# Second MLP of a fused attention and two-MLP kernel: stores moved to GpSimd's queue, weight requests reordered, lower halves of split operands made later

## The chip, the cores and the metric
The kernel runs on one core of a Trainium2 chip. The metric is the device time of one execution in microseconds (us), median of several runs. TensorE (PE; its weight loads are PEld), VectorE (DVE), ScalarE (ACT) and GpSimd (POOL) each work through a queue of their own in order. SyncE (SP) computes nothing: its queue holds requests for transfers (DMA). A request that waits for a semaphore holds back all requests behind it on its queue. The transfers themselves run on the core's 16 DMA engines.

## The reference, cut to what matters
```
x  = attention(q, k, v)            # 4 x 576 tokens = 2304, 512 wide
h1 = x @ w1_in                     # first MLP, d_ff 2048
y  = (h1 - tanh(h1)) @ w1_out
h2 = y @ w2_in                     # second MLP: this is where the change is
g  = h2 * tanh(softplus(h2))       # Mish
out = g @ w2_out
```
All is float32. The kernel reaches float32 precision on TensorE by splitting each operand into an upper half (what is left after rounding to a shorter format) and a lower half (the difference), and by three products: upper x upper, upper x lower, lower x upper. The upper half comes from ScalarE (a copy, or Mish itself, written in the short format), the lower half from a subtract on DVE.

## The kernel before, in words
The second MLP uses Strassen-like 2x2 block products. The 2304 tokens are four blocks u = 0 to 3: 768 tokens, then three times 512. The 2048 hidden columns are eight slices j = 0 to 7. A group k = 8u + j handles one slice for one block; there are 32, one after the other. A group has seven products with W2in's block j (`product`, line 1052; six matmuls each, in the order 2, 0, 1, 4, 3, 5, 6 from block 1 on), each followed by some of the second-layer units of the group before (`o2_units`: 12 of three matmuls in block 0, seven of six matmuls after it, named 11, 22, S1, S3, 12, S2, S4). `UNITS` (line 1298) says how many units follow which product. Behind each product stand the steps of `combine` (line 1110): ScalarE or DVE take the product from one of two PSUM banks (products 2, 4, 6 in one; 0, 1, 3, 5 and unit S4 in the other), add, apply Mish, and split the result into halves (`mish`, `halved`).

While block 0 runs (groups 0 to 7), the weights are prepared beside it by `w2_cycles` (line 165). Raw float64 rows are loaded (`load_raw`), joined to float32, summed and split. The products' operands W2in go to DRAM by `keep` (line 241, 1.8 MB in two stores a slice, tensor w2s), the sums for W2out by `t_lo` (line 223, four stores of 256 KB a slice, tensor w2t). From block 1 on each group loads W2in's block for the next group (`w2c_load`, line 332, two loads of 1024 and 768 KB, tile P) and W2out's sums for its own slice (`t_load`, line 342, four loads of 256 KB, tile w). P has buffers for two groups.

The outputs of a block of tokens leave at its end: block 0 by `o_evict` (line 1177, six stores), the others by `out_sums` (line 1213: adds on DVE, four stores). All these requests are on SP's queue, in the order in which the code stands. The operands of the next block are made by `y_prep` (line 960) in steps spread over some groups.

The whole second MLP stands in a stretch whose order is exactly the order of the code (line 1328). `group` (line 1301) emits a product, its units, then asks `bg2` (line 1511) for what runs beside it, and then `parts` takes turns between `combine` and these, from yield to yield; a yield is thus a place where another stream's instruction may come between. `bg2` gets the place p of the product in its group, 0 to 6. These lines set the places of the loads:
```
if u and p == 0:
    t_load(j)
if k + 1 >= NJ and k + 1 < NU * NJ and p == 1:
    w2c_load((k + 1) % NJ)
```

Of the kernel before, what the change touches and what calls it, by code (L numbers as in the profile page):

```python
# [15 lines left out]
ACTF = mybir.ActivationFunctionType  # L16
# [13 lines left out]
def kernel(  # L30
# [134 lines left out]
    def w2_cycles():  # L165
# [57 lines left out]
        def t_lo(j, i):  # L223
            if 0 <= j < NJ and (j, i) in ts_todo:
                ts_todo.remove((j, i))
                t, h = ts[j][i], TW[0][:, i, :]
                V.tensor_tensor(out=t.bitcast(F32R), in0=t, in1=h, op=ALU.subtract)
                for x, src in ((0, h), (1, t)):
                    nc.sync.dma_start(out=w2t[j][:, 2 * i:2 * i + 2, x, :], in_=src.rearrange("p (n c) -> p n c", n=2))

        def hi(W, i, src):
            A.activation(out=W[:, i:i + src.shape[1], 0, :], in_=src, func=ACTF.Copy)
# [8 lines left out]
        def keep(j):  # L241
            for q in range(2):
                n = 4 - q
                nc.sync.dma_start(out=w2s[j][q][:, 0:n, :], in_=f32(W2c[j][q][:, 0:n].rearrange("p n t c -> p n (t c)")))

        fetch("a", 0)
        fetch("b", 0)
# [712 lines left out]
    def y_prep(u):  # L960
        C = C3 if u else C2

        def load(kh, th):
            t = (p2["yl"].tile([128, 2, C2], F32, tag="yl", name="yl")[:, :, 0:C] if u and th else raw_f32()[
                :, 0:2 * C].rearrange("p (a n) -> p a n", a=2))
            n0 = 0
            while n0 < C:
                i, o = divmod(token0(u) + th * C + n0, HS)
                n = min(C - n0, HS - o)
                nc.sync.dma_start(out=t[:, :, n0:n0 + n], in_=ys[i][:, 2 * kh:2 * kh + 2, o:o + n])  # L970
                n0 += n
            return t

        def sub(o, x, y, op=ALU.subtract):
            V.tensor_tensor(out=o, in0=x, in1=y, op=op)  # L975

        def tile(p):
            if p < 6:
                if u == 0:
                    t = p2["yk"].tile([128, 2, 2, C2], F32R, tag="yk", name="yk")  # L980
                    Y[u, p] = [t[:, 0], t[:, 1]]
                elif u == 1:
                    t = p2["yk"].tile([128, 3, 2, C3], F32R, tag="yk", name="yk")
                    Y[u, p] = [t[:, 0], t[:, 1]]
                    free.append(t[:, 2])
                else:
                    if p == 2:
                        for n in ORDER[1][:-1]:
                            free.extend(Y[u - 1, n])
                    Y[u, p] = [free.pop(0) for _ in range(2)]  # L990
            elif u:
                if not Y6:
                    Y6.append(AT_p.tile([128, 2, 2, C3], F32R, tag="AT", name="AT"))
                    OUT.append(AT_p.tile([128, 2, 2 * C3], F32, tag="AT", name="AT"))
                Y[u, p] = [Y6[0][:, 0], Y6[0][:, 1]]
            else:
                Y[u, p] = [AT_p.tile([128, 2, C2], F32R, tag="AT", name="AT") for a in range(2)]

        def halves(p, t):
            if (u, p) not in Y:  # L1000
                tile(p)
            y = Y[u, p]
            for a in range(2):
                A.activation(out=y[a][:, 0, :], in_=t[:, a], func=ACTF.Copy)
                yield 0
                sub(y[a][:, 1, :], t[:, a], f32(y[a][:, 0, :]))

        a21, a22 = load(0, 1), load(1, 1)
        s1, s2 = [p2["yf"].tile([128, 2, C2], F32, tag="yf", name="yf")[:, :, 0:C] for _ in range(2)]
        yield 1  # L1010
        if u == 0:
            a11, a12 = load(0, 0), load(1, 0)
            for p in range(6):
                tile(p)
        sub(s1, a21, a22, ALU.add)
        yield 1
        if u:
            a11, a12 = load(0, 0), load(1, 0)
            yield 1
            sub(s2, s1, a11)  # L1020
            yield 1
            sub(a21, a11, a21)
            yield 1
            order = ((0, a11), (2, a12))[::1 if u == 1 else -1] + ((1, s2), (4, s1), (3, a21), (5, a22), (6, s2))
        else:
            yield from halves(5, a22)
            yield 1
            sub(a21, a11, a21)
            yield 0
            sub(s2, s1, a11)  # L1030
            yield 1
            order = ((3, a21), (0, a11), (1, s2), (2, a12), (4, s1), (6, s2))
        for p, t in order:
            yield from halves(p, t)
            if p == (1 if u else 2):
                sub(s2, a12, s2)
            yield 1


    ORDER = ((0, 2, 1, 4, 3, 5, 6), (2, 0, 1, 4, 3, 5, 6))  # L1040
    evict, YK, free = [], [], []
    Y6, OUT, TW, HB, Q, XG, late_sums, late_acc = [], [], [], [], {}, [], [], []

    def bank_of(k, p):
# [42 lines left out]
    def mish(k, n, src=None):  # L1087
        x = xs[k, n]
        h = x if src is None else src
        gg = operand(k, n)  # L1090
        A.activation(out=gg[:, 0, :], in_=h, func=ACTF.Mish)  # L1091
        A.activation(out=x, in_=h, func=ACTF.Mish)  # L1092
        yield 0
        V.tensor_tensor(out=gg[:, 1, :], in0=x, in1=f32(gg[:, 0, :]), op=ALU.subtract)  # L1094
        yield 0

    def halved(k, n, x):
        gg = operand(k, n)
        split(x, gg[:, 0, :], gg[:, 1, :], V)
        return 0  # L1100

    def sums_12(k):
# [7 lines left out]
    def combine(k, p):  # L1110
        t = bank_of(k, p)

        def add(o, x, y):
            V.tensor_tensor(out=o, in0=x, in1=y, op=ALU.add)  # L1114

        def keep(n):
            A.activation(out=x_of(k, n), in_=t, func=ACTF.Copy)  # L1117

        if p == 0:
            keep("11")  # L1120
        if p == (0 if k >= NJ else 2):
            add(xs[k, "11"], xs[k, "11"], bank_of(k, 2))
            yield from mish(k, "11")
        elif p == 1:
            keep("12")
            while late_sums:
                yield from late_sums.pop()
        elif p == 3:
            keep("22")
            add(xs[k, "22"], xs[k, "22"], bank_of(k, 4))  # L1130
            yield from mish(k, "22")
        elif p == 5:
            if k < NJ:
                x_of(k, "21")
                yield from mish(k, "21", t)
            else:
                y = x_of(k, "21")
                A.activation(out=y, in_=t, func=ACTF.Mish)
        elif p == 6:
            add(xs[k, "12"], xs[k, "12"], t)  # L1140
            while late_acc:
                late_acc.pop()()
            if k >= NJ:
                y = xs[k, "21"]
                add(xs[k, "22"], y, xs[k, "22"])
                yield from mish(k, "12")
                yield halved(k, "S1", xs[k, "22"])
                V.tensor_tensor(out=y, in0=xs[k, "11"], in1=y, op=ALU.subtract)  # L1148
                yield halved(k, "S3", y)
                late_sums.append(sums_12(k))  # L1150
            else:
                yield from mish(k, "12")
        yield 1

    def o2_units(k):
# [21 lines left out]
    def o_evict(u, tt):  # L1177
        o = p2["st"].tile([128, 512], F32, tag="y", name="y") if tt not in (5, 0) else OUT[0][:, tt // 5]
        if tt in (4, 1):
            V.tensor_copy(out=o, in_=ops[u, tt])  # L1180
        else:
            A.activation(out=o, in_=ops[u, tt], func=ACTF.Copy)
        nc.sync.dma_start(out=out[tt * 128:tt * 128 + 128, :], in_=o)

# [26 lines left out]
    def out_sums(u, n, j):  # L1213
# [4 lines left out]

        def store(o, th, ch):
            r0 = token0(u) + 2 * 128 * th  # L1220
            nc.sync.dma_start(out=out[r0:r0 + 256, C3 * ch:C3 * ch + C3].rearrange("(t p) c -> p t c", p=128),
                              in_=o.rearrange("p (t c) -> p t c", t=2))

        def staged(x, m):
# [100 lines left out]
    def pipeline(bg, bg2):  # L1325
        for s in range(0, SWITCH, 2):
            pair(s, bg)
        with tc.manual_schedule():
# [12 lines left out]
            for k in range(NU * NJ):  # L1341
                group(k, bg2)
            parts(late_sums)
            for _ in o2_units(NU * NJ - 1):
                pass
            late_acc.pop()()
# [55 lines left out]
    if True:  # L1402
# [109 lines left out]
        def bg2(k, p):  # L1512
            u, j = divmod(k, NJ)
            mix = []
            if u == 0:
                mix.append(gens["cv"])
            if u and p == 0:
                t_load(j)
            if k + 1 >= NJ and k + 1 < NU * NJ and p == 1:
                w2c_load((k + 1) % NJ)  # L1520
            if u + 1 < NU and (j, p) == YPREP[u > 0][0]:
                gens["y"] = vec_only(y_prep(u + 1))
            if u + 1 < NU and (j, p) in YPREP[u > 0] or j == 0 and p < (1, 3, 1, 1)[u]:
                mix.append(gens["y"])
            return mix
# [46 lines left out]
```

## Time and profile before
| | us |
|---|---|
| runs, median (lowest, highest; 3) | 850.51 (848.61, 850.86) |
| profiled execution | 852.7 |
| its span | 850.9 |
| TensorE busy in the span | 788.5 (93%) |
| DVE, ScalarE, GpSimd busy | 658.7, 559.0, 192.9 |

The second MLP's products start at 424.5 us and its last matmul ends at 841.3 us; the rest of the span is the last output adds and stores. The mean granted TensorE clock is 0.987 of full speed. A matmul's row shows its own duration, but matmuls overlap, so a row of six lasts longer than the distance to the next row. A transfer's request on SP is a row of "SPq"; what it moves lands later. In a row of the timeline the bracket gives the idle time of the engine just before it and what ended it.

### The profile page before, as it was taken

The page shows a single profiled execution, that of the slowest core. Times are in us where ns is not written, and L with a number is a line of the kernel's source. Part 1 is how long each engine was busy: PE and PEld are TensorE (multiplying, and loading weights), DVE is VectorE, ACT ScalarE, POOL GpSimd, SP SyncE. Part 2 cuts the span into 40 slices and gives each one's busy share as a digit, 9 for nine tenths or more (in the row PEclk, how much of TensorE's full clock was granted, in tenths as well). Part 3 has the DMA queues.
Part 4 walks back from the last instruction along what each step waited for, and adds up shares of the span by engine and source line. Part 5 has one row for each costly group of instructions (what it writes and reads, how often), then busy time and mean ns, then how long its engine had stood idle before and what let it go on. Part 6 is the DMA issues. An engine that isn't in the chain of part 4 may idle for free.

```text
span 850.9 us, 16979 instructions
## 1 busy us (share of the span) xinstructions
PE 788.5 (93%) x6241; PEld 699.4 (82%) x6241; DVE 658.7 (77%) x1421; ACT 559.0 (66%) x1330; POOL 192.9 (23%) x215
## 2 busy tenths in 40 slices
PE   7898999999999999989989999988998799988995
PEld 4556787888878987779978988887998799887994
DVE  7789999997799868898878888854667656674556
ACT  4677877887778777867777777653555454644552
POOL 0000038765777657722300000000000000000000
PEclk9999999999999999999999999998999999999998
DMA  8798924404142002312059999979886599739861
GB/s 266 268 313 300 336 81 148 135 2 141 50 158 76 2 30 100 103 50 103 26 194 355 317 299 361 302 260 325 297 306 226 190 349 331 240 121 361 302 210 50
DMA packets 82322, 172.00 MB, mean 202 GB/s; under 512 B 8768, under 2 KB 54336, under 8 KB 78144
## 3 DMA queue, kind: packets, MB, share of 16 engines
q1 hardware_dynamic: 82240, 170.93, 58.0%
q8 instruction: 49, 0.80, 0.4%
q14 instruction: 33, 0.27, 0.1%
HBM read 134.20 MB, written 36.70 MB: 201 GB/s over the span
## 4 chain that ended last, share of the span: by engine, by line
PE 47%; DVE 23%; ACT 12%; DMA 10%; issue 5%; POOL 2%; SPq 0%; DVEq 0%; ACTq 0%
PE h L1050 15%; DMA P<-w2s 5%; PE y L1050 5%; PE y L939 3%; PE y L943 3%; PE y L940 3%; PE m L1050 2%; ACT gg L116 2%; DVE tc L857 2%; DVE yk L975 2%; PE y L1171 2%; PE y L1170 2%; PE y L1172 2%; DVE tb L861 1%; DMA raw<-in_w1o_dram 1%
## 5 line engine op out<-in xcount | busy, mean ns | idle before, releaser
L1050 PE MATMUL h<-yk,P 128*128 128x256 f32 (+1 forms) x1152 | 185.8, 300 | 24.1 <-DMA P<-w2s 13.2
L1050 PEld LDWEIGHTS h<-yk,P 128*128 128x128 f32 x1152 | 164.4, 192 | 34.2 <-DVE gg L117 8.1
L939 PE MATMUL y<-gg,w 128*128 128x288 f32 x448 | 132.6, 311 | 4.6 <-ACT raw L948 3.5
L940 PE MATMUL y<-gg,w 128*128 128x288 f32 x448 | 125.8, 295 | 0.0
L911 POOL TENSOR_SCALAR mk<-es 128x288 uint8<-128x288 f32 x80 | 78.6, 982 | 139.2 <-DVE yv L671 115.5
L939 PEld LDWEIGHTS y<-gg,w 128*128 128x128 f32 x448 | 84.1, 188 | 23.7 <-issue 15.2
L943 PE MATMUL y<-gg,w 128*128 128x288 f32 x448 | 96.0, 295 | 0.0
L940 PEld LDWEIGHTS y<-gg,w 128*128 128x128 f32 x448 | 84.3, 188 | 0.7 <-issue 0.2
L1050 PE MATMUL y<-w,gg 128*128 128x256 f32 x576 | 83.6, 288 | 0.9 <-issue 0.7
L1050 PEld LDWEIGHTS y<-w,gg 128*128 128x128 f32 x576 | 76.2, 196 | 1.9 <-ACT x L1117 0.8
L943 PEld LDWEIGHTS y<-gg,w 128*128 128x128 f32 x448 | 71.8, 188 | 0.2
L152 ACT ACTIVATE top<-raw 128x512 f16<-128x512 bf16 x64 | 48.9, 783 | 13.4 <-DVE raw L184 3.8
L1094 DVE TENSOR_TENSOR gg<-x,gg 128x384 fp32r<-128x384 f32 (+1 forms) x48 | 23.6, 491 | 34.9 <-ACT x L1092 34.0
L117 POOL TENSOR_TENSOR gg<-tc,gg 128x288 fp32r<-128x288 f32 (+1 forms) x45 | 39.8, 892 | 39.7 <-ACT gg L116 36.1
L117 POOL TENSOR_TENSOR gg<-tb,gg 128x288 fp32r<-128x288 f32 (+1 forms) x44 | 40.4, 922 | 31.7 <-ACT gg L116 23.9
L834 PE MATMUL h<-AT,P 128*128 128x288 f32 x144 | 43.0, 299 | 2.9 <-DVE ta L924 2.9
L909 ACT ACTIVATE es<-h 128x288 f32<-128x288 f32 x80 | 32.1, 402 | 18.5 <-PE h L836 15.6
L914 ACT ACTIVATE qs<-qs,bias_c 128x288 f32<-128x288 f32 x80 | 42.7, 534 | 1.3
L835 PE MATMUL h<-AT,P 128*128 128x288 f32 x144 | 42.4, 295 | 0.0
L836 PE MATMUL h<-AT,P 128*128 128x288 f32 x144 | 42.4, 295 | 0.0
L116 ACT ACTIVATE gg<-w 128x256 fp32r<-128x256 f32 x48 | 20.0, 417 | 28.0 <-DVE w L1148 19.9
L1091 ACT ACTIVATE gg<-x 128x256 fp32r<-128x256 f32 (+1 forms) x40 | 18.4, 461 | 27.9 <-DVE x L1114 27.9
(249 smaller groups left out, 1957.0 us busy)
## 6 DMA issues: line engine op xcount, KB each, us to landing
P<-w2s SPq DMA_DIRECT2D x24, 1024.0 KB, 7.0
w<-w2t SPq DMA_DIRECT2D x96, 256.0 KB, 4.7
P<-w2s SPq DMA_DIRECT2D x24, 768.0 KB, 8.4
w<-w1s SPq DMA_DIRECT2D x24, 512.0 KB, 4.5
w2s<-P SPq DMA_DIRECT2D x8, 1024.0 KB, 5.6
raw<-in_w1i_dram SPq DMA_DIRECT2D x16, 511.8 KB, 4.9
raw<-in_w1o_dram SPq DMA_DIRECT2D x16, 511.8 KB, 4.8
raw<-in_w2i_dram SPq DMA_DIRECT2D x16, 511.8 KB, 5.1
```

The lines of the kernel that those rows point to most:

```text
L116: A.activation(out=H, in_=src, func=ACTF.Copy)
L117: eng.tensor_tensor(out=L, in0=src, in1=f32(H), op=ALU.subtract)
L152: A.activation(out=top[:, :, 1], in_=raw.bitcast(BF16)[:, :, 2], func=ACTF.Copy)
L834: mm(p, P[:, g, 0, c], AT[:, g, 0, :], start=(g == 0), stop=False)
L835: mm(p, P[:, g, 0, c], AT[:, g, 1, :], start=False, stop=False)
L836: mm(p, P[:, g, 1, c], AT[:, g, 0, :], start=False, stop=(g == NG - 1))
L911: G.tensor_scalar(out=mk, in0=e, scalar1=FT, scalar2=None, op0=ALU.is_ge)
L914: A.activation(out=q, in_=q, func=ACTF.Square, scale=FB, bias=bias_c[:, 0:1])
L939: mm(yps[d], w[:, 0, c], gg[:, 0, :], start=(f == 0), stop=False)
L940: mm(yps[d], w[:, 1, c], gg[:, 0, :], start=False, stop=False)
L943: mm(yps[d], w[:, 0, c], gg[:, 1, :], start=False, stop=(f == NF - 1))
L1050: mm(*args, **kw, skip_group_check=True)
```

## The change
Four things are edited.
- The stores of `t_lo`, `keep` and `o_evict`, and those of `out_sums` except for the last block, are issued by GpSimd.
- In `bg2`, `w2c_load` stands ahead of `t_load`, at place 0 and not 1.
- The lower halves of the second layer's operands go through a list: `low_later` notes one and makes the one noted before it; `low_now` makes the oldest. In product 6's steps the order of the adds changes accordingly.
- `y_prep`'s `halves` asks for both upper halves and then makes both lower halves, with a yield after each.

```
@@ t_lo, keep
-                    nc.sync.dma_start(out=w2t[j][:, 2 * i:2 * i + 2, x, :], ...)
+                    nc.gpsimd.dma_start(out=w2t[j][:, 2 * i:2 * i + 2, x, :], ...)
-                nc.sync.dma_start(out=w2s[j][q][:, 0:n, :], ...)
+                nc.gpsimd.dma_start(out=w2s[j][q][:, 0:n, :], ...)
@@ y_prep: halves
             for a in range(2):
                 A.activation(out=y[a][:, 0, :], in_=t[:, a], func=ACTF.Copy)
                 yield 0
+            for a in range(2):
                 sub(y[a][:, 1, :], t[:, a], f32(y[a][:, 0, :]))
+                yield 0
@@ mish, halved
         A.activation(out=x, in_=h, func=ACTF.Mish)
         yield 0
+        low_later(gg, x)
+        yield 0
+    def low_later(gg, x):
+        lows.append((gg, x))
+        if len(lows) > 1:
+            low_now()
+    def low_now():
+        gg, x = lows.pop(0)
         V.tensor_tensor(out=gg[:, 1, :], in0=x, in1=f32(gg[:, 0, :]), op=ALU.subtract)
-        yield 0
     def halved(k, n, x):
         gg = operand(k, n)
-        split(x, gg[:, 0, :], gg[:, 1, :], V)
+        A.activation(out=gg[:, 0, :], in_=x, func=ACTF.Copy)
+        low_later(gg, x)
@@ combine, p == 6
             add(xs[k, "12"], xs[k, "12"], t)
+            if k >= NJ:
+                y = xs[k, "21"]
+                low_now()
+                add(xs[k, "22"], y, xs[k, "22"])
             while late_acc:
                 late_acc.pop()()
             if k >= NJ:
-                y = xs[k, "21"]
-                add(xs[k, "22"], y, xs[k, "22"])
-                yield from mish(k, "12")
+                V.tensor_tensor(out=y, in0=xs[k, "11"], in1=y, op=ALU.subtract)
+            yield from mish(k, "12")
+            if k >= NJ:
                 yield halved(k, "S1", xs[k, "22"])
-                V.tensor_tensor(out=y, in0=xs[k, "11"], in1=y, op=ALU.subtract)
                 yield halved(k, "S3", y)
                 late_sums.append(sums_12(k))
-            else:
-                yield from mish(k, "12")
@@ o_evict, out_sums: store
-        nc.sync.dma_start(out=out[tt * 128:tt * 128 + 128, :], in_=o)
+        nc.gpsimd.dma_start(out=out[tt * 128:tt * 128 + 128, :], in_=o)
-            nc.sync.dma_start(out=out[r0:r0 + 256, ...], ...)
+            (nc.gpsimd if u < NU - 1 else nc.sync).dma_start(out=out[r0:r0 + 256, ...], ...)
@@ pipeline, after the last group
             parts(late_sums)
+            while lows:
+                low_now()
@@ bg2
+            if k + 1 >= NJ and k + 1 < NU * NJ and p == 0:
+                w2c_load((k + 1) % NJ)
             if u and p == 0:
                 t_load(j)
-            if k + 1 >= NJ and k + 1 < NU * NJ and p == 1:
-                w2c_load((k + 1) % NJ)
```

SP's queue from the last preparation of weights to group 10, before. P<-w2s are `w2c_load`'s loads, w<-w2t `t_load`'s, w2t<- the stores of `t_lo`, out_dram<- those of the outputs.
```order
L229 DMA w2t_100<-w 128x2x256
L229 DMA w2t_100<-y 128x2x256
L344 DMA w<-w2t_93 128x2x256 x4
L336 DMA P<-w2s_0_79 128x2048
L336 DMA P<-w2s_1_80 128x1536
L1183 DMA out_dram<-y 128x512 x2
L1183 DMA out_dram<-AT 128x512 x2
L1183 DMA out_dram<-y 128x512 x2
L344 DMA w<-w2t_94 128x2x256 x4
L336 DMA P<-w2s_0_81 128x2048
L336 DMA P<-w2s_1_82 128x1536
```
The same queue now, from the load for group 8 on:
```order
L336 DMA P<-w2s_0_77 128x2048
L336 DMA P<-w2s_1_78 128x1536
L336 DMA P<-w2s_0_79 128x2048
L336 DMA P<-w2s_1_80 128x1536
L344 DMA w<-w2t_93 128x2x256 x4
L336 DMA P<-w2s_0_81 128x2048
L336 DMA P<-w2s_1_82 128x1536
L344 DMA w<-w2t_94 128x2x256 x4
```
No store is left between the loads, and each pair of P stands ahead of the four loads of w that it followed.

DVE at the end of block 2 (group 23, products 3 to 6), before. The operands' lower halves are the rows of L1094; L1114 are adds on the products, L1217 adds of the output.
```order
L1114 TENSOR_TENSOR w<-w,h 128x256
L1094 TENSOR_TENSOR gg<-w,gg 128x256
L1217 TENSOR_TENSOR AT<-AT,m 128x512
L1217 TENSOR_TENSOR y<-AT,m 128x512
L1217 TENSOR_TENSOR AT<-AT,y 128x512 x2
L1114 TENSOR_TENSOR w<-w,h 128x256
L1217 TENSOR_TENSOR top_136<-top_136,h 128x512
L1114 TENSOR_TENSOR w<-w 128x256
```
Now, with L1107 for the lower halves, L1127 and L1231 for the adds:
```order
L1127 TENSOR_TENSOR w<-w,h 128x256
L1107 TENSOR_TENSOR X<-w,X 128x256
L1231 TENSOR_TENSOR AT<-AT,m 128x512
L1231 TENSOR_TENSOR y<-AT,m 128x512
L1231 TENSOR_TENSOR AT<-AT,y 128x512 x2
L1127 TENSOR_TENSOR w<-w,h 128x256
L1107 TENSOR_TENSOR gg<-w,gg 128x256
L1127 TENSOR_TENSOR w<-w 128x256
```
The lower half ahead of the output adds is now that of an operand asked for earlier (X, for unit S4); the one that stood there follows the add of product 6. The four output adds keep their place.

## Rows read from the trace of the kernel before
**Rows 1.** Stretches: busy us of PE, PEld, DVE, ACT, POOL; PEclk; DMA; GB/s
```profile
450.00:540.00 90.00, 90.00 (x450) 80.66 (x448) 77.81 (x148) 68.96 (x129) 0.00 (x0) 1.00 0.94 319
...
568.00:580.40 12.40, 12.40 (x98) 11.85 (x97) 6.73 (x17) 6.78 (x18) 0.00 (x0) 1.00 0.62 192
...
785.00:825.00 40.00, 40.00 (x338) 40.00 (x337) 24.01 (x61) 21.42 (x57) 0.00 (x0) 1.00 0.84 288
```
**Rows 2.** Waits of the whole span: us in total, times, longest us
```profile
PE h L1050 <- DMA P<-w2s: 13.2, 5, 4.2
...
PEld h L1050 <- ACT w L1138: 4.7, 11, 1.0
```
**Rows 3.** Timeline, groups 7 to 8: start us, us, what [idle before, releaser]
```profile
535.27 1.23 PE L1050 MATMUL h<-AT,P 128*128 128x384 f32 x6
...
544.57 2.57 SPq L336 DMA_DIRECT2D P<-w2s  x2
...
553.64 0.55 DVE L1114 TENSOR_TENSOR u<-u,h 128x384 f32<-128x384 f32 x1
...
555.24 1.04 PE L1050 MATMUL h<-yk,P 128*128 128x256 f32 x4 [2.39 <-DMA P<-w2s]
```
**Rows 4.** Timeline, groups 8 to 10
```profile
565.40 3.25 SPq L1183 DMA_DIRECT2D out_dram<-y  x2
...
568.06 0.89 PE L1050 MATMUL h<-AT,P 128*128 128x256 f32 x6
...
576.81 0.90 SPq L336 DMA_DIRECT2D P<-w2s  x2
...
584.61 1.62 PE L1050 MATMUL h<-yk,P 128*128 128x256 f32 x6 [4.21 <-DMA P<-w2s]
```
**Rows 5.** Timeline, end of block 1
```profile
671.62 1.22 SPq L336 DMA_DIRECT2D P<-w2s  x2
...
679.26 0.92 PE L1050 MATMUL h<-yk,P 128*128 128x256 f32 x6 [2.70 <-DMA P<-w2s]
```
**Rows 6.** Timeline, end of block 2
```profile
773.07 0.92 PE L1050 MATMUL h<-yk,P 128*128 128x256 f32 x6 [3.61 <-DMA P<-w2s]
```
**Rows 7.** Stretches behind the standstills, columns as in rows 1
```profile
555.20:558.00 2.80, 2.76 (x10) 2.50 (x11) 2.14 (x6) 1.85 (x6) 0.00 (x0) 0.54 0.77 262
...
584.60:588.00 3.40, 3.39 (x16) 3.40 (x17) 0.00 (x0) 0.00 (x0) 0.00 (x0) 0.50 1.06 374
588.00:592.00 4.00, 4.00 (x29) 4.00 (x29) 1.18 (x3) 1.86 (x5) 0.00 (x0) 0.81 1.02 411
...
662.00:668.00 6.00, 3.81 (x20) 3.61 (x20) 5.39 (x12) 1.67 (x4) 0.00 (x0) 0.72 0.13 45
...
773.10:778.00 4.90, 4.90 (x29) 4.90 (x30) 0.42 (x1) 0.88 (x3) 0.00 (x0) 0.65 1.09 400
```
**Rows 8.** Timeline, DVE and PE at the end of group 23
```profile
754.35 0.42 DVE L1094 TENSOR_TENSOR gg<-w,gg 128x256 fp32r<-128x256 f32 x1 [0.93 <-ACT w L1092]
...
757.33 0.41 DVE L1114 TENSOR_TENSOR w<-w,h 128x256 f32<-128x256 f32 x1
...
757.80 0.97 PE L1050 MATMUL h<-yk,P 128*128 128x256 f32 x6 [2.21 <-DVE w L1114]
```
**Rows 9.** Timeline, DVE after the last group
```profile
840.05 0.43 DVE L117 TENSOR_TENSOR X<-w,X 128x256 fp32r<-128x256 f32 x1 [0.48 <-ACT X L116]
```
**Rows 10.** Transfers: KB each, median us to landing; line 229: min/median/max
```profile
P<-w2s SPq DMA_DIRECT2D x24, 1024.0 KB, 7.0
...
P<-w2s SPq DMA_DIRECT2D x24, 768.0 KB, 8.4
...
DMA to landing us min/median/max: 3.1/5.5/8.4
```
**Rows 11.** Timeline, a store of w2t and the next writes of its buffer
```profile
495.81 1.83 SPq L229 DMA_DIRECT2D w2t<-y  x1
...
505.11 0.88 DVE L239 TENSOR_TENSOR y<-raw,y 128x256 f32<-128x256 f32 x2
```

More of the change, by code (lines that the diff above doesn't have):

```diff
@@ L228, in t_lo @@
                 for x, src in ((0, h), (1, t)):
-                    nc.sync.dma_start(out=w2t[j][:, 2 * i:2 * i + 2, x, :], in_=src.rearrange("p (n c) -> p n c", n=2))
+                    nc.gpsimd.dma_start(out=w2t[j][:, 2 * i:2 * i + 2, x, :], in_=src.rearrange("p (n c) -> p n c", n=2))
         def hi(W, i, src):
@@ L243, in keep @@
                 n = 4 - q
-                nc.sync.dma_start(out=w2s[j][q][:, 0:n, :], in_=f32(W2c[j][q][:, 0:n].rearrange("p n t c -> p n (t c)")))
+                nc.gpsimd.dma_start(out=w2s[j][q][:, 0:n, :], in_=f32(W2c[j][q][:, 0:n].rearrange("p n t c -> p n (t c)")))
         fetch("a", 0)
@@ L1040 @@
     ORDER = ((0, 2, 1, 4, 3, 5, 6), (2, 0, 1, 4, 3, 5, 6))
-    evict, YK, free = [], [], []
+    evict, YK, free, lows = [], [], [], []
     Y6, OUT, TW, HB, Q, XG, late_sums, late_acc = [], [], [], [], {}, [], [], []
@@ L1220, in store @@
             r0 = token0(u) + 2 * 128 * th
-            nc.sync.dma_start(out=out[r0:r0 + 256, C3 * ch:C3 * ch + C3].rearrange("(t p) c -> p t c", p=128),
+            (nc.gpsimd if u < NU - 1 else nc.sync).dma_start(out=out[r0:r0 + 256, C3 * ch:C3 * ch + C3].rearrange("(t p) c -> p t c", p=128),
                               in_=o.rearrange("p (t c) -> p t c", t=2))
```

## Prediction
> **What bounds the kernel now.** I read the page first, then the table of stretches, the waits of TensorE, and then the timeline at each place where TensorE stood still.
>
> The table of stretches splits the second MLP in three [rows 1]. While the first eight token groups run (450 to 540 us) TensorE is busy all 90 us, DVE 77.81 and the DMA engines 0.94 of the time; 450 matmuls in 90 us at 78 a group make 15.6 us a group. In the late groups (785 to 825 us) TensorE is again busy throughout: 338 matmuls in 40 us at 84 a group, so 9.9 us a group and 0.71 for each of its 14 runs of six. Between these and at the end of each block of tokens it stands still. The waits name what ends most of that: five waits for W2in's blocks, 13.2 us in all [rows 2]. So the sum is made over single standstills, not over busy shares.
>
> Four of these have one shape. SP's queue holds W2in's next blocks behind something slow.
> - Product (7,6) ends at 536.5 us (535.27 plus 1.23), which frees the buffers, yet SP asks for the blocks at 544.57, behind stores that wait for DVE; TensorE starts at 555.24 after 2.39 us of waiting [rows 3].
> - SP holds the six output stores of block 0 from 565.40 on, asks at 576.81, and TensorE waits 4.21 us [rows 4].
> - At the end of block 1 output stores stand in front again, the blocks are asked for at 671.62, and TensorE waits 2.70 us [rows 5], with the fifth wait right behind it (13.2 - 2.39 - 4.21 - 2.70 - 3.61 = 0.29).
> - The same at the end of block 2: 3.61 us [rows 6].
>
> After these the granted clock falls to its lower level, 1.2 GHz, for a while [rows 7]: 0.50 and 0.81 after the second, 0.65 after the fourth, 0.54 after the first. After the DVE stall near 663 us it is 0.72. After the 2.70 us stall no lower stretch follows in these rows.
>
> **The change part by part.** The sum is made against the profiled execution's own 852.7 us (span 850.9 and 1.8 around it), which stands 2.2 us above the median of the runs, 850.51.
>
> *Stores on GpSimd, and W2in's blocks asked for ahead of W2out's, one place earlier.* SP's queue then holds only loads whose buffers come free by TensorE. What each standstill leaves:
> - First: asked for soon after the release at 536.5 us, the blocks have some 15 us; they landed in 7.0 and 8.4 us at the median [rows 10]. Next late is DVE: the add of product (7,6), at 553.64 and done 0.55 later at 554.19, frees the bank that TensorE then writes [rows 3]. As it stands that gives 555.24 - 554.19 = 1.05 us; without any such wait 2.39. DVE loses one 0.8 us wait ahead of that add by the third part of the change, so I take 1.8.
> - Second: 4.21, all of it. Third: 2.70 + 0.29. Fourth: 3.61. The bank is free in time there, since the wait ended on the blocks alone. Sum of the four: 1.8 + 4.21 + 2.99 + 3.61 = 12.6; bounds 11.9 and 13.2.
> - The clock: a stretch at granted clock g loses (1 - g) of its length. 3.40 x 0.50 + 4.00 x 0.19 = 2.5 after the second, 4.90 x 0.35 = 1.7 after the fourth, 2.80 x 0.46 = 1.3 after the first [rows 7]. All three go with the standstill: 5.5; bound below 0.
>
> The price of a store issued by GpSimd isn't in this trace; the nearest rows are SP's stores to the same tensor, landing in 3.1 to 8.4 us [rows 10]. GpSimd's busy time is 0.00 in these stretches [rows 1], so the issue itself delays nobody, and I take a landing like SP's, that is 0. From below: the raw loads of W2 are no longer behind stores, but TensorE is busy throughout there, so no gain. From above: who waits is DVE, whose subtract writes the buffer of a store asked for at 495.81 only at 505.11 [rows 11]. Landings up to 9.3 us cost nothing. What happens beyond is a rival below.
>
> The rows show the DMA engines 0.62 busy between 568 and 580.4 us, at 192 GB/s, which is 310 GB/s at full use, while TensorE ran into its longest wait [rows 1]. The Trainium skill ("DMA: Bandwidth & Descriptors", section "Issuing engines are not separate DMA queues") says that DMAs started by SP, ScalarE and GpSimd run on the same 16 engines and interleave, and that spreading them saves only the time to initiate them. By that rule the six stores (1.6 MB, 5.1 us at 310 GB/s) push the blocks, asked for when product (8,6) ends (568.06 + 0.89 = 569.0, [rows 4]), back: 569.0 + 8.4 + 5.1 = 582.5 against 580.4, so 2.1 of the 4.21 us would stay. By the row's idle share they fit. The trace can't decide, as it has one queue.
>
> *W2out's blocks behind W2in's.* They were asked for during the group before, as their readers finished; now they are asked for at a group's start, for use one group later. The first is read after four more runs of six, 2.8 us into the next group, so 9.9 + 2.8 = 12.7 us after. Both loads are 2.88 MB; at 288 GB/s for a share of 0.84, that is 343 GB/s [rows 1], they need 8.4 us and some 2 us to land: 10.4. Cover 2.3 us; cost 0. In return W2in's blocks no longer stand behind four loads that wait for TensorE one by one.
>
> *Lower halves behind the next upper half.* The number of DVE and ScalarE instructions stays. What goes are DVE's waits of 0.93 us for ScalarE's second Mish. Where TensorE is full this buys nothing. It counts in three places:
> - End of blocks 1 and 2. DVE has low half (after 0.93 us of waiting, at 754.35), four adds of the output, and only then at 757.33 the add that frees the bank; TensorE waits 2.21 us [rows 8]. In the new order the low half at that place is an older one whose ScalarE part is long done. So 0.93 us less at each of the two: 1.9. At the end of block 1 the low clock after it (6.00 x 0.28 = 1.7 [rows 7]) goes with a shorter wait or doesn't; I take 0.8. Bounds: 0, and 4.4 + 1.7 for all of both waits.
> - Groups in which the next block's operands are made: TensorE waits 4.7 us in 11 pieces for ScalarE's Mish of the bank [rows 2]. ScalarE's queue has the same work, but its partner DVE is earlier; I take half, 2.3; bounds -1 (DVE's work for the next operands now stands in another order) and 4.7.
> - The end. The ten output adds start one behind the other after the last low half, which ends at 840.05 + 0.43 = 840.5 [rows 9]. With the waits of 0.48 us for ScalarE at the last low halves gone (three or four), the adds start 1.4 to 1.9 us earlier; I take 1.6. Bounds 0 and 1.9.
>
> *Sum.* 12.6 + 5.5 + 1.9 + 0.8 + 2.3 + 1.6 = 24.7 us. 852.7 - 24.7 = 828.0; from the median it would be 825.8. I keep the 2.2 us as allowance for waits that the removed ones hid, and say 828. All lower bounds together (11.9 + 0 + 0 - 1 + 0 = 10.9 off) give 841.8; all upper ones (13.2 + 5.5 + 6.1 + 4.7 + 1.9 = 31.4) 821.3, from the median 819.1.
>
> **Rivals.**
> 1. *Something else is late where the blocks were.* DVE and ScalarE used the standstills to catch up; without them the bank adds and upper halves may end each place one or two us later, the clock may fall all the same and the small waits stay. For it: at the first standstill DVE's add is only 1.05 us away [rows 3], and the clock fell after a DVE wait of some 2.2 us too, and no row shows after how short a one it would not. Against it: between 785 and 825 us the same chains keep TensorE full [rows 1]. Only the lower bounds of the sum are left: 852.7 - 11.9 = 840.8, some 840.
> 2. *Slower: stores land too late in the first stage.* GpSimd's queue takes keep's 1.8 MB and W2out's 1 MB in each group of 15.6 us, DMA is 0.94 busy there, and raw loads now run beside the stores and not behind them. DVE's subtract waits for the second store's landing. DVE has (90 - 77.81) x 15.6 / 90 = 2.1 us to spare per group [rows 1]. So from 9.3 + 2.1 = 11.4 us to landing TensorE loses, eight times; from 11.4 + 24.7 / 8 = 14.5 us the kernel is slower than before. At 16 us: 828 + 8 x 4.6 = 865. Against it: 8.4 us at most so far [rows 10]. The Trainium skill ("SBUF — State Buffer", section "SBUF: two separate sides") tells of one way to it, a GpSimd-issued DMA whose descriptors can't be written while DVE copies fp32 from SBUF to SBUF in a two-port mode; no run here shows that, and this stage has no such copy.
> 3. *Unchanged or slower: W2out's blocks late in every late group.* If the two loads together need over 12.7 us, each of some 23 groups waits for the excess; from 12.7 + 24.7 / 23 = 13.8 us it eats all. That needs a rate under 2.88 MB / 11.8 us = 244 GB/s, and 343 is what the row gives. At 14.5 us: 828 + 23 x 1.8 = 869.
> 4. *The move does nothing*: the blocks would arrive as late as before because DMA, not the queue, was the limit. Against it: 0.62 of DMA time in front of the longest wait. 850.
>
> **How the numbers follow.** My case 0.64 (821 to 835), rival 1 0.20, rival 2 0.07, rival 3 0.05, rival 4 0.04. Within 0.3% (848.0 to 853.1) is about what a measurement of this kernel can't tell from no change. Faster: my case, rival 1 and a mild form of 3, 0.86; same: rival 4 and a little of the others, 0.05; slower: 0.09. The range goes from all upper bounds, 820, to rival 1 with 2 us for what I can't see, 842; outside it are the three last cases and a little below.
>
> **What would show it.** Right: waits for DMA of W2in's blocks under 2 us in all; SP's requests for them at a group's start, within 1 us of the end of the last product; one or no low-clock stretch between 550 and 840 us; DVE's waits for the second Mish gone; the ten last adds starting well before TensorE ends. Wrong: waits of DVE for a DMA between 450 and 550 us; waits for W2out's blocks; TensorE less than full in the late groups; or standstills at the same places that now end on DVE's or ScalarE's bank reads.

## The result: 1.0% faster, where 2.6% was forecast

The changed kernel took 841.99 us at the median of four runs (840.56 to 843.62), the kernel before 850.68 (848.61 to 853.01): ratio 0.990, 95% interval 0.986 to 0.993. Run again beside other kernels it was 0.992 (0.988 to 0.995). The forecast was 828, with a range from 820 to 842, so the time lies at its slow end. The profiled execution has a span of 838.8 us, 12.1 less than before.

TensorE's waits of the changed kernel from 424 us to the end (us in total, times, longest):
```profile
PE h L1052 <- DVE w L1127: 13.2, 9, 5.1
PE h L1052 <- DVE u L1127: 3.4, 2, 2.8
PE h L1052 <- ACT u L1130: 1.9, 2, 1.3
...
PE h L1052 <- ACT w L1151: 0.4, 2, 0.2
```
The five waits for W2in's blocks, 13.2 us [rows 2], are gone, as forecast. In their place stand, by chance again, 13.2 us of waits for one DVE line, L1127, the add that empties a bank. Before, its waits at the ends of blocks 1 and 2 were 2.2 us each (the second stands in [rows 8]); now one wait is 5.1 us long. So the first question is what DVE itself was waiting for. The timeline of the changed kernel at that place (SP's requests, DVE, PE) answers it:
```profile
601.01 1.06 SPq L336 DMA_DIRECT2D P<-w2s  x2
602.17 2.16 SPq L344 DMA_DIRECT2D w<-w2t  x4
604.43 4.05 SPq L970 DMA_DIRECT2D yl<-ys  x4
...
607.54 0.42 DVE L1107 TENSOR_TENSOR gg<-x,gg 128x256 fp32r<-128x256 f32 x1 [0.33 <-ACT gg L1111]
615.04 0.69 DVE L975 TENSOR_TENSOR yf<-yl 128x512 f32<-128x512 f32 x1 [7.08 <-DMA yl<-ys]
615.65 0.41 DVE L1127 TENSOR_TENSOR w<-w,h 128x256 f32<-128x256 f32 x1
...
616.12 1.65 PE L1052 MATMUL h<-AT,P 128*128 128x256 f32 x6 [5.08 <-DVE w L1127]
```
The subtract at L975 is a step of `y_prep`: it reads ys, from which the operands of the next block of tokens are made. Its load stands on SP behind W2in's blocks and W2out's, which are asked for at the group's start. DVE works in order, so it stops for 7.08 us with the bank's add behind the subtract, and TensorE stops 5.08 us. Next, the same requests in the kernel before:
```profile
605.32 2.00 SPq L970 DMA_DIRECT2D yl<-ys  x4
607.42 0.89 SPq L336 DMA_DIRECT2D P<-w2s  x2
...
614.34 0.69 DVE L975 TENSOR_TENSOR yf<-yl 128x512 f32<-128x512 f32 x1
```
There ys was asked for ahead of W2in's blocks, 9 us before its reader. The view of that tile has the landing times of its four loads (min/median/max), first before, then after:
```profile
DMA to landing us min/median/max: 2.9/3.3/3.6
```
```profile
DMA to landing us min/median/max: 6.8/9.0/9.4
```
In the changed kernel three of the four are asked for by 605.89, 2 us before DVE's turn at 607.96, and land 8.8 to 9.4 us later, right behind the last of W2out's blocks (613.28). So what makes them late is above all the 2.9 MB in front of them, which the DMA engines move first, and less the moment of the request. DVE also comes earlier: its turn is 4.9 us behind the start of the units of group 11, and not 6.7.

The same happens one block later, at 702.6 us, for 3.54 us. The granted clock falls behind each of these, as it fell behind the old ones [rows 7]. Stretches of the changed kernel behind its first standstill (at 554.5 us) and the two new ones, columns as in rows 1:
```profile
559.00:563.00 4.00, 4.00 (x17) 3.39 (x16) 3.04 (x8) 1.60 (x6) 1.43 (x2) 0.69 0.90 332
...
616.00:620.00 4.00, 3.88 (x20) 3.88 (x21) 2.49 (x7) 2.35 (x6) 0.00 (x0) 0.57 0.33 92
...
704.00:708.00 4.00, 1.88 (x9) 1.88 (x10) 1.55 (x4) 1.11 (x3) 0.00 (x0) 0.60 0.65 261
708.00:712.00 4.00, 4.00 (x22) 4.00 (x22) 2.68 (x7) 1.67 (x4) 0.00 (x0) 0.54 0.75 231
```
The first standstill, forecast to shrink from 2.39 to some 0.6 us, is there with another releaser. GpSimd's request for a store, DVE and PE in the changed kernel:
```profile
544.59 0.73 POOL L229 DMA_DIRECT2D w2t<-y  x1
...
555.86 0.89 DVE L239 TENSOR_TENSOR y<-raw,y 128x256 f32<-128x256 f32 x2 [1.79 <-DMA w2t<-y]
556.67 0.55 DVE L1127 TENSOR_TENSOR u<-u,h 128x384 f32<-128x384 f32 x1
...
557.27 1.02 PE L1052 MATMUL h<-yk,P 128*128 128x256 f32 x6 [2.77 <-DVE u L1127]
```
DVE may write tile y only when the store asked for at 544.59 has landed, 11 us later. Over the first groups this is DVE's largest wait. Here are its waits from 440 to 560 us, then the transfers' median landing from 440 to 553 us, then the same transfer before:
```profile
DVE y L239 <- DMA w2t<-y: 13.0, 8, 3.2
```
```profile
w2t<-y POOLq DMA_DIRECT2D x14, 256.0 KB, 7.8
```
```profile
w2t<-y SPq DMA_DIRECT2D x14, 256.0 KB, 4.3
```
These medians mix two kinds of store. A slice has two stores of y, and the second is asked for behind the two stores of `keep` (1.8 MB). Before, the first kind took 3.4 to 3.9 us and the second 4.7 to 7.8 (median 7.2). In the changed kernel the first takes 2.6 to 8.1 us, the second 7.4 to 11.3 (median 10.2), and seven of DVE's eight waits are for the second.

And what the third part was to bring did come: the wait at the end of block 1 is 1.01 us and not 2.2, with no low clock behind it, and the last ten adds start 1.7 us before the end of TensorE's last unit, not 0.7:
```profile
663.34 0.98 PE L1052 MATMUL h<-yk,P 128*128 128x256 f32 x6 [1.01 <-DVE w L1127]
```
```profile
828.50 0.69 DVE L1231 TENSOR_TENSOR AT<-AT,y 128x512 f32<-128x512 f32 x1
```
```profile
829.31 0.87 PE L1052 MATMUL h<-w,X 128*128 128x256 f32 x6
```

Where the time comes and goes is seen best by setting profiles side by side at the moments when the second-layer units of a group start. Each column is that moment less the one of the kernel before, in us; the last six are experiments told of below. Lows stands for the third part of the change (lower halves late), stores for the first, W2in first for the second.

| units of group | before | changed | lows alone | lows + output stores | all stores alone | W2in first alone | changed, stores on SP | changed, ys first |
|---|---|---|---|---|---|---|---|---|
| 0 | 442.9 | -1.8 | 0.0 | -0.7 | +0.9 | +1.1 | +2.3 | -1.1 |
| 8 | 570.9 | +2.0 | -3.9 | -4.5 | +9.9 | +4.2 | +4.2 | +1.2 |
| 11 | 607.6 | -4.6 | -4.5 | -9.4 | +7.8 | -1.3 | -1.5 | -5.4 |
| 14 | 641.1 | +1.0 | -7.2 | -12.1 | +7.8 | +5.1 | +3.8 | -8.1 |
| 17 | 680.0 | -5.6 | -10.5 | -18.6 | +4.8 | +2.2 | -2.8 | -14.7 |
| 20 | 711.0 | -0.9 | -11.0 | -19.4 | +4.2 | +8.7 | +2.8 | -15.5 |
| 23 | 745.6 | -2.5 | -13.6 | -22.4 | +4.3 | +9.9 | +0.4 | -18.4 |
| 26 | 785.4 | -10.8 | -16.6 | -30.6 | -1.2 | +5.5 | -6.6 | -26.7 |
| span's end | 850.9 | -12.1 | -17.9 | -31.6 | -0.9 | +5.4 | -7.9 | -28.1 |

From group 0 to 8 the changed kernel loses 3.8 us, at each of three block ends it gains 6.6 to 8.3, and in groups 11 to 14 and 17 to 20, where ys is loaded, it gives 5.6 and 4.7 back (the third part alone gains 2.7 and 0.5 there). A second profile of the changed kernel gives these steps within 0.4 us. Between groups 1 and 6, where the first block runs evenly, the changed kernel loses 3.1 us, the first part alone 5.5, and the kernels with the stores on SP none.

### The profile page after: what moved, and what is told of

Its sections match the earlier page's. It is cut to its first block, busy times and chain, and to the rows that moved or that the text cites. A ratio compares the mean times of both kernels' runs of the same rounds, so it can differ in the third digit from the quotient of the medians.

```text
span 838.8 us, 16921 instructions
## 1 busy us (share of the span) xinstructions
PE 784.2 (93%) x6240; PEld 699.3 (83%) x6241; DVE 653.0 (78%) x1421; ACT 559.5 (67%) x1330; POOL 233.6 (28%) x277
## 5 line engine op out<-in xcount | busy, mean ns | idle before, releaser
L939 PEld LDWEIGHTS y<-gg,w 128*128 128x128 f32 x448 | 84.7, 189 | 23.4 <-issue 15.2
L1052 PE MATMUL y<-w,gg 128*128 128x256 f32 x576 | 80.9, 283 | 0.7 <-DVE gg L1107 0.7
L1052 PEld LDWEIGHTS y<-w,gg 128*128 128x128 f32 x576 | 73.9, 191 | 1.2 <-DVE gg L1107 0.9
L1127 DVE TENSOR_TENSOR w<-w,h 128x256 f32<-128x256 f32 x48 | 20.1, 418 | 48.9 <-PE h L1052 26.3
L152 ACT ACTIVATE top<-raw 128x512 f16<-128x512 bf16 x64 | 47.9, 780 | 11.8 <-DVE w L157 3.9
L1235 POOL DMA_DIRECT2D out_dram<-y x4 | 2.9, 718 | 177.2 <-DVE y L1231 177.2
L1052 PE MATMUL h<-AT,P 128*128 128x256 f32 (+1 forms) x192 | 32.7, 308 | 9.7 <-DVE w L1127 9.6
```

What stands on the lines that cost most here:

```text
L152: A.activation(out=top[:, :, 1], in_=raw.bitcast(BF16)[:, :, 2], func=ACTF.Copy)
L939: mm(yps[d], w[:, 0, c], gg[:, 0, :], start=(f == 0), stop=False)
L1052: mm(*args, **kw, skip_group_check=True)
```

## The experiments

Theory A: the ys loads' place in SP's queue takes back most of the gain. Rival B: the queue is innocent; the DMA engines are full, or the new order on DVE is to blame. Further, each part was undone or done alone. "Before" on the same chip had medians of 852.43 (first four kernels), 850.37 (next four) and 850.67 (last four).

**ys loads on GpSimd** (the changed kernel, blocks 2 and 3):
```
-  nc.sync.dma_start(out=t[:, :, n0:n0 + n], in_=ys[i]...)
+  (nc.gpsimd if u > 1 else nc.sync).dma_start(out=t[:, :, n0:n0 + n], in_=ys[i]...)
```


> The changed kernel, but the loads of the next block's ys (L970, for blocks 2 and 3) are issued by GpSimd, whose queue is empty there. Theory A (SP's queue: these loads now stand behind W2in's and W2out's blocks, which wait for TensorE): both new standstills, 5.08 and 3.54 us, and the low clock after them (3.41 and 6.83 us at half rate, 5.1 us) go, DVE's wait of 7.08 us for yl is gone, 842.0 - 12 = 830 us (828 to 833). Theory B (the queue is not it; the 16 DMA engines are full of W2in's and W2out's 2.8 MB, or DVE's new order is to blame): the loads land late from GpSimd too, DVE still waits 3 us or more for them, 838 to 842 us.


Measured 826.63 us, ratio 0.970 (0.965 to 0.975), 1.4 us under the range of theory A. Its waits of TensorE from 540 us on:
```profile
PE h L1052 <- DVE u L1127: 3.7, 1, 3.7
PE h L1052 <- DVE w L1127: 3.6, 6, 1.0
...
```
No wait for ys is left; the waits for L1127 fall from 13.2 to 3.6 us. GpSimd asks for ys at 573.4 us, 33 us ahead of the reader, so this run moves the moment as well as the queue.

**ys first, all on SP.** This one keeps the queue and changes the place alone:
```
+ late_y = u in (1, 2) and j in (4, 5)
- if k + 1 >= NJ and k + 1 < NU * NJ and p == 0: w2c_load(...)
+ if k + 1 >= NJ and k + 1 < NU * NJ and p == 0 and not late_y: w2c_load(...)
  if u and p == 0: t_load(j)
+ if p == 1 and late_y: w2c_load(...)
```


> The changed kernel, with W2in's blocks asked for one product later and behind W2out's and ys in the two groups of a block in which ys is loaded (groups 4 and 5 of blocks 1 and 2), all on SP as in the changed kernel. Theory A (the place in SP's queue): no wait of DVE for ys of over 1 us, both standstills go, 842 - 15 = 827 us (825 to 831). Theory B (the ys loads must leave SP's queue altogether, or DMA's share decides): 835 to 842 us.


Measured 824.65 us, ratio 0.970 (0.967 to 0.973), just under the range of theory A. In its timeline ys is asked for at 599.93, ahead of W2in's blocks, and lands in 4.8 us:
```profile
599.93 1.96 SPq L970 DMA_DIRECT2D yl<-ys  x4
602.07 1.08 SPq L336 DMA_DIRECT2D P<-w2s  x2
```
In four groups one request stands one product later and behind ys, and that is worth 17 us. Theory A holds: it is the place in the queue, which is also the place in the order of the transfers. B falls.

**Second part undone** (the two lines of `bg2` as before):


> The changed kernel with the second part undone: W2in's blocks are asked for one product later and behind W2out's, as before; stores stay on GpSimd and the lower halves late. Theory A: the ys loads are ahead of W2in's blocks again, the two standstills and their low clock go; the stores no longer hold SP, so W2in's blocks come in time too: 829 to 834 us, faster than the changed kernel. Theory B, and also if W2in's place in the queue was what cured the four standstills: TensorE waits 2 to 4 us for W2in's blocks again at the block ends, 842 to 850 us.


Measured 830.06 us, 0.974 (0.970 to 0.978). From group 8 on it runs as the kernel with ys on GpSimd does (14 to 15 us gained on the changed kernel's profile in either); only up to group 8 is it 5.2 us later. So in blocks 1 to 3, once the stores are off SP, W2in's blocks need not stand first.

**Third part undone** (`mish`, `halved`, product 6 and `halves` as before):


> The changed kernel with its third part undone: lower halves made at once, as before. If that part is worth what its shortened waits show (1.2 us at each of two block ends, 1 us at the tail, 1 to 2 us of small ones, and a low clock after the first block end, 1.7 us): 842.0 + 6 = 848 us (845 to 850). Rival: the reordering brought DVE to its read of ys too early and so made the new standstills; without it they shrink to nothing and the time is 832 to 838 us.


Measured 861.51 us, 1.010 (1.006 to 1.014): slower than before. TensorE's largest waits from 540 us on are below. The third part is worth 19.5 us here by the medians, 17 by the ratios, against 6 expected. The rival is wrong too: the two standstills at ys stay (4.05 and 4.15 us), so the new order on DVE did not make them.
```profile
PE h L1050 <- DVE w L1114: 15.7, 10, 4.2
PE h L1050 <- DVE u L1114: 3.3, 1, 3.3
PE y L1050 <- ACT y L1182: 3.2, 1, 3.2
...
```
Without it, the end of block 0, where TensorE used to wait 4.21 us for W2in's blocks, now waits 3.2 us for ScalarE's copy of an output.

**Stores back on SP** (first part undone):


> The changed kernel with the first part undone: all stores issued by SP again. If GpSimd's stores are what cost 3.8 us over the first nine groups: that comes back, DVE's waits for the landing of W2out's halves (13.0 us, 8 times) go to under 2 us. At the block ends SP again holds W2in's blocks behind output stores: 8 to 12 us of standstills and 3 to 5 us of low clock; the ys standstills stay. Together 842.0 - 3.8 + 11 = 849 us (845 to 855). Rival: asking for W2in's blocks first is enough by itself, 836 to 840 us.


Measured 843.80 us, 0.989 (0.985 to 0.994), between the two theories and no different from the changed kernel. TensorE's largest waits from 540 us on:
```profile
PE h L1052 <- DVE w L1127: 13.4, 9, 5.1
PE h L1052 <- DVE u L1127: 4.3, 1, 4.3
PE y L1052 <- DMA w<-w2t: 1.7, 3, 0.8
```
The ys waits stay (12.9 us of DVE), and the steady groups 1 to 6 are as before. But no wait for W2in's blocks returns, although the output stores are on SP: asked for first, the blocks no longer stand behind them. By the table the three block ends gain 19 us, against 20 in the kernel below that moves the output stores and keeps the old order, and 7 with the third part alone. So either part removes these standstills.

**Third part alone:**


> The kernel before with the third part alone (lower halves made behind the next request for an upper half); all stores on SP, W2in's blocks behind W2out's, as before. If the four standstills for W2in's blocks (12.9 us and some 7 us of low clock) are the queue's alone, they stay and only the block ends, the small waits and the tail get better: 852 - 6 = 846 us (843 to 849). Rival: the parts don't add, and the standstills were as much DVE's and ScalarE's, which this part brings forward: 835 to 842 us. Second rival: nothing without the others, 850 to 854 us.


Measured 836.46 us, 0.984 (0.982 to 0.987): faster than the whole change. TensorE's waits from 540 us on:
```profile
PE h L1052 <- DMA P<-w2s: 10.3, 4, 3.8
PE h L1052 <- DVE w L1127: 3.6, 6, 1.0
PE h L1052 <- DVE u L1127: 0.9, 1, 0.9
...
```
The rival holds: the parts don't add. The standstills for W2in's blocks at the three block ends stay (10.3 us). The first one is gone: with DVE earlier, SP's stores of W2out's sums and the request behind them are earlier too (542.83 against 544.57 [rows 3]), and no low clock follows the 0.9 us that remain.

**First part alone:**


> The kernel before with the first part alone (all stores on GpSimd). Theory: no wait for W2in's blocks in the late blocks, but at the same places TensorE then waits for ScalarE's and DVE's, which were as late (3.17 us for ScalarE's eviction at the end of block 0 and 2.2 us at the ends of blocks 1 and 2, as in the variant without the third part); the first nine groups lose 3 to 5 us to stores that land late: 861.5 - 16 (no ys standstills there) = 845 us (842 to 850). Rival: the standstills were the queue's alone, 15 us go: 836 to 840 us.


Measured 849.90 us, 0.999 (0.997 to 1.001), no difference. It is at the upper edge of what was expected. All waits for W2in's blocks are gone, and nothing is won in all: behind group 8 the kernel gains 10.8 us, but up to there it has lost 9.0 (the table). At the end of block 0 ScalarE is late in place of the blocks; the 2.2 us for DVE at the other two block ends were there before. TensorE's largest waits from 540 us on:
```profile
PE h L1050 <- DVE w L1114: 6.1, 7, 2.2
PE h L1050 <- DVE u L1114: 4.8, 1, 4.8
PE y L1050 <- ACT y L1182: 2.9, 1, 2.9
...
```

**Second part alone:**


> The kernel before with the second part alone (W2in's blocks asked for first in a group). Theory: the ys loads of blocks 2 and 3 stand behind W2in's and W2out's blocks, DVE waits 6 to 7 us for them, TensorE 4 us twice and its clock falls: slower than before, 858 us (853 to 862). Rival: as the request stands ahead of the output stores the four standstills shrink and pay for it, 846 to 852 us.


Measured 857.42 us, 1.008 (1.005 to 1.010): slower than before. No wait for W2in's blocks is left here either, and the three block ends gain 13 us (the table); the two stretches with ys give 13 back. DVE's waits for ys in it:
```profile
DVE yf L975 <- DMA yl<-ys: 9.3, 2, 5.1
...
DVE yf L975 <- DMA raw<-ys: 2.1, 2, 1.6
```

**Third part and the output stores only:**
```
  t_lo, keep:         nc.sync     (as before)
  bg2:                t_load, then w2c_load at p == 1 (as before)
- o_evict, out_sums:  nc.sync
+ o_evict, out_sums:  nc.gpsimd   (out_sums: but for the last block)
```


> The kernel before with the third part (lower halves late) and, of the first part, only the output stores on GpSimd; W2's own stores stay on SP and W2in's blocks stay behind W2out's. Theory: the three standstills for W2in's blocks that the third part alone leaves (3.30, 3.28 and 3.76 us and 5 us of low clock) come from output stores in SP's queue, and nothing else of the first two parts is needed: 836.5 - 14.5 = 822 us (820 to 825). Rival: asking for W2in's blocks first is what is needed, the standstills stay at 2 us or more each: 828 to 836 us.


Measured 820.98 us, 0.965 (0.962 to 0.968). All its waits of TensorE from 540 us on:
```profile
PE h L1052 <- DVE w L1127: 3.6, 6, 1.0
PE y L1052 <- ACT y L1196: 1.3, 1, 1.3
PE h L1052 <- DVE u L1127: 0.9, 1, 0.9
PE y L1052 <- DVE gg L1107: 0.7, 1, 0.7
```
The granted clock is 1.00 in every stretch from 540 to 785 us. Six stores of block 0 and four each of blocks 1 and 2 are enough of the first part, and nothing of the second is needed.

**A third buffer for y** (with ys on GpSimd; yl made smaller for the room):
```
- ("st", 2)      p2["yl"].tile([128, 2, C2], ...)
+ ("st", 3)      p2["yl"].tile([128, 2, C3], ...)
```


> The first variant (next block's ys loads issued by GpSimd, 826.6 us) with a third buffer for the tiles y that W2out's sums are stored from (room made by a smaller yl). Theory: in the first nine groups DVE waits 12.7 us in 7 pieces for a store's landing before it may write the tile; with one tile more those waits and the 3.73 us standstill at 551.6 us with its low clock (1.7 us) go: 826.6 - 5 = 821.5 us (820 to 824). Rival: DMA is the limit there, the next wait (W2in's first blocks, raw loads) takes their place: 825 to 828 us.


Measured 820.83 us, 0.966 (0.964 to 0.969). DVE's waits for the stores are gone from its list and the first standstill is 0.89 us. With this and the queue mended, the change as it stands is worth 30 us.

**Stores on SP, raw loads on GpSimd** (with ys on GpSimd), to tell why the stores land late:


> The first variant (826.6 us) with the two kinds of DMA of the first nine groups swapped: stores of W2in's and W2out's parts issued by SP, raw loads of W2 by GpSimd; both still run beside one another. Theory C (the stores land late, 7.6 us at the median for w2t<-y against 4.3 before, because loads now run beside them on the same DMA engines): they land as late, 7 us, DVE's waits for them stay at 9 us or more, the same time within 2 us. Theory D (a store that GpSimd issues is itself slower): landing 4 to 5 us, DVE's waits under 5 us, 2 us faster, 824 to 825 us.


Measured 835.61 us, 0.983 (0.980 to 0.987), 9 us slower than without the swap; DVE waits more for the store, 17.6 us. The store of tile y lands in 5.3 us at the median, which alone would speak for theory D. But that median lies between the two kinds: the first lands in 2.2 to 4.5 us, the second in 6.0 to 11.8 (median 9.2). Without the swap the second kind takes 7.4 to 12.2 us (median 9.9). So beside loads SP's stores land nearly as late as GpSimd's, which speaks for theory C. The longest wait, 6.2 us, follows a pair that stands on SP behind ys loads that wait for buffers (four of them hold SP from 510.13 for 4.86 us). The kernel before has the same hold (510.20, 5.20 us) and no such wait: there the store landed in 4.7 us, here in 9.5. Neither theory's time came out, and the requests moved in time as well; this stays open.

**The changed kernel again:**


> The changed kernel once more, beside the three variants on the same chip: 0.990 of the kernel before, the same two standstills at DVE's read of ys.


Measured 842.31 us, 0.992 (0.988 to 0.995); its standstills at ys are 5.13 and 3.58 us.

## Why the prediction was wrong

The step that failed is "W2out's blocks behind W2in's", with its "cost 0", and the sentence that "SP's queue then holds only loads whose buffers come free by TensorE". It asked whether the four W2out loads that are moved behind would still come in time. They do: TensorE has no wait for them in the changed kernel. But SP's queue holds a third kind of request there, `y_prep`'s loads, which the code issues in the same place p = 0 and which the move also puts behind W2in's blocks. Measured, that is worth 17 us (842 against 824.65). The profile of before held the warning: those loads were asked for at 605.32, with W2in's request right behind, and read at 614.34. A cover of 9 us cannot take a request that waits for TensorE's product plus 2.9 MB in front of it. One sign of being wrong that the prediction named did show, DVE waiting for a DMA between 450 and 550 us (11.0 us for the stores), but the larger loss, behind 600 us, had no sign.

Step by step:
- *Second, third and fourth standstill, 15.0 us with their clock.* Right, in place and nearly in size. With the third part in both, moving the output stores alone gains 13.2 us behind group 8 (31.6 - 4.5 less 17.9 - 3.9). The prediction took both parts for one cure; either is enough, as the new order alone and the new order with the stores on SP have no wait for the blocks either. The reason given, that the bank is free in time "since the wait ended on the blocks alone", does not follow: without the third part TensorE waits 2.9 to 3.2 us there for ScalarE.
- *First standstill, 1.8 us and 1.3 of clock.* Wrong: 2.77 us and a low clock, now by a store. The third part alone does what the first two were to do there. (The product that ends at 536.5 us is product 6 of group 6; product (7,6) starts at 550.92. The buffers are read rightly.)
- *A store by GpSimd costs nothing.* Wrong by 3.8 us in the changed kernel (group 0 to 8, first standstill included), 9.0 us when done alone. (With the stores back on SP 1.9 us of the loss remain, at the first standstill.) It is rival 2 in a mild form: its bound was the landing beyond which TensorE loses, 11.4 us. The median of all these stores is 7.8, but that of the second kind is 10.2, and DVE, earlier by the third part, wants the buffer 7.2 to 9.5 us after the request and not 9.3. One buffer more removes the loss.
- *Lower halves, 6.6 us.* Mis-sized: alone they give 13.9 us by the medians; in the profiles it is 13.9 behind group 8 and 3.9 up to there. The 0.93 us taken off each block end was 1.2, the low clock behind the end of block 1 (1.7 us, taken as 0.8) went wholly, the small waits fell by 1.9 us in each block (taken as 1.15), the tail shrank by 1.0 (taken as 1.6). That is 8.9 of the 13.9 us behind group 8; the rest was not traced. What was not seen is the 3.9 us, through SP's stores that wait for DVE.
- *The sum.* Up to group 8 the forecast had a gain of 3.1 us and the profile shows a loss of 3.8: 6.9 missed. Behind group 8 it had 21.6. The kernel with ys first gains 29.3 there, 7.7 more, mostly by the lower halves; the changed kernel gains 14.1, so ys took 15.2. So 24.7 - 6.9 + 7.7 - 15.2 = 10.3 us, and 1.8 lie ahead of group 0, where single profiles differ by some us: together the 12.1 of the two profiles (the medians give 8.7). The kernels with only the ys loads mended came out at 824.65 and 826.63, near the 828 forecast, but by errors of both signs.
- *Rival 1* has the right time, 840, for another reason. Its mechanism, DVE and ScalarE late at the same places, is what the kernels without the third part show at the end of block 0 (2.9 to 3.2 us for ScalarE). It is the smaller part of why the first part alone gains nothing: 10.8 us came behind group 8 in place of 15.0, and the late stores took 9.0. In the changed kernel the third part takes it away. That 840 is near the measured time is luck.
- *Rivals 3 and 4* did not occur. The Trainium skill ("DMA: Bandwidth & Descriptors", section "Issuing engines are not separate DMA queues") says that requests of different engines run on the same 16 DMA engines; by the estimate made from that, output stores and loads beside one another would have left 2.1 us of the second standstill. The trace agrees with this: in the kernel with only output stores moved, the DMA engines are 1.02 busy from 564.7 to 576.6 us, and W2in's blocks land late, 11.9 and 13.1 us after their requests (13.5 by that estimate; 7.0 and 8.4 at the median before [rows 10]):
```profile
L336 SPq DMA_DIRECT2D P<-w2s x2: 715/836/958, 564.7 to 565.5; - x2
...
DMA to landing us min/median/max: 11.9/12.5/13.1
```
TensorE does not wait, because the product that reads the second block starts 13.3 us after its request (at 578.76, 0.1 us after the landing). So the time until the reader decided, with next to nothing to spare, and not the idle share of the row.

## What to carry to other kernels

When a request that waits is moved forward on an in-order queue, list every kind of request that is issued between its old and its new place, and behind it, and for each its reader's time less its own: the one with the smallest cover pays. A wait that ends on a transfer says nothing about how late the other engines are; before counting it as gain, look for the instruction that would end it next, and mend that first. And try the parts of a change alone: here the third part gave more than all three, and the other two cured the same standstills, each with a loss of its own: the new order at ys, W2's stores in the first groups. The output stores alone brought the cure without either.

## What was not expected of the hardware

- The clock's fall multiplies small standstills. Waits of TensorE of 1.0 us (block ends with late lower halves) and 1.3 us (third part and output stores) left the granted clock at 1.00; one of 1.34 us, in the kernel with the third part undone, was followed by 4 us at 0.66. Of the 38 waits of 2.1 to 5.6 us behind 440 us in all the traces, 31 were followed by a stretch at the lower level, 1.2 GHz, and seven, of 2.2 to 3.1 us, were not. The waits for W2in's blocks in the third part alone (three of 3.1 to 3.8 us and a small one, 10.3 us in all) cost 13.2 us with what followed them.
- The same 256 KB store landed later where loads ran beside it: the second kind took 7.2 us at the median in the kernel before, 9.2 issued by SP with loads of GpSimd beside it, and 9.9 issued by GpSimd with loads of SP beside it. The company makes most of the difference in these runs; as requests moved in time too, it is not settled.
